# The joints of four interleaved attention layers: loads, row buffers and last rows moved

## The chip, the cores and the metric

The kernel runs on one core of one Trainium2 chip. The core has five engines: TensorE (PE, matrix products into PSUM), VectorE (DVE), ScalarE (ACT), GpSimd (POOL) and SyncE (SP), which here only issues DMAs. The metric is the device time of one execution in microseconds (us); less is better. A profile shows one execution on a time scale that starts with the span.

## The reference

2048 tokens of width 640 pass through four residual layers, A, B, A, B. Each adds the layer's output to its input, after a normalization of rows.

```python
x = x + _A_ref(_layernorm(x), A_wq, A_wk, A_wv, A_wo, A_beta)
x = x + _B_ref(_layernorm(x), B_mem0, B_Wq, B_Wk, B_Wv, B_Wo, B_seg_len)
x = x + _A_ref(_layernorm(x), A_wq, A_wk, A_wv, A_wo, A_beta)
x = x + _B_ref(_layernorm(x), B_mem0, B_Wq, B_Wk, B_Wv, B_Wo, B_seg_len)

# A: 32 heads of 20, four segments of 512 tokens
for s in range(4):
    p = softmax(q @ k.T * scale + mask)                 # causal, within the segment
    a_mem = (phi(q) @ M) / (phi(q) @ z + 1e-06)          # memory of the segments before
    o = sigmoid(beta) * a_mem + (1 - sigmoid(beta)) * (p @ v)
    M, z = M + phi(k).T @ v, z + sum(phi(k))
# then o @ wo

# B: 32 heads of 128, 64 steps of 32 tokens, 8 memory rows
for s in range(64):
    h = concat(mem, x[32 * s:32 * s + 32])               # 40 rows
    p = softmax(mask(q @ k.T * scale))                   # q, k, v from h
    o = (p @ v) @ Wo
    mem, out = o[:8], o[8:]                              # mem goes into the next step
```

## The kernel before

**Layer A** (`layer_A`) takes a segment of 512 tokens and 8 groups of 4 heads, 32 groups in all. Four row tiles of 128 tokens are loaded (`seg_load`, a_xt), normalized (`seg_norm`: bn_stats, a_ln_rstd, a_xn), transposed on PE (`seg_tr`, a_tps to a_xnT) and projected (`proj_q`: a_QP, `proj_kv`: a_KV). `unread` issues PE products a_W that nobody reads; they keep PE at work while it waits. The output of a segment is stored by `out_stage_b`: the product a_YP, the residual row a_xr added on DVE (a_xnew), the sum stored in f32 (xres), cast to bf16 (a_xnb) and stored again (xres_bf). PE's order is that of the program; `KeyOrder` orders DVE, ACT and POOL by due times, `K.base` plus an entry of `A_LAGS`. The padded weights of layer A (a_wq_pad, a_wkv) are made by DVE casts in the first layer, kept in HBM (`keep_padded`) and loaded from there in the second A layer.

**Layer B** (`layer_B`) has the query and key weights resident. The value weights (W.wv) and output weights (b_wo, eight loads of 640 KB) are loaded for each B layer. For the token rows, which don't depend on the memory, queries, keys and values are made ahead in tiles, `tail_unit` (b_tail, evacuated to b_tu, stored through b_QKd) and `vtail_unit` (b_vtail, stored through b_VTd, loaded again as b_Vth). A step s makes Ka, Qa, Kb, Qb for the eight memory rows, transposes them (b_TPak, b_TPaq, b_TPbk, b_TPbq), forms scores (b_SP), softmax on DVE, ACT and POOL, the transposed probabilities (b_PTa, b_PTb), PV (b_OTP, evacuated to b_OTsb), and the output product b_OPS. b_OPS covers the 24 leading tokens of the step and the 8 memory rows; the 8 last tokens of the steps are put aside (b_OTdef) and multiplied for four steps together in `od_chunk` (b_OPSd). `x_out` adds two halves of the product to the residual rows on DVE (b_XO, b_XOd for the put-aside rows, b_XOe for those of the last four steps) and stores. The queries of the memory rows give the next memory; after the last step there is none. All engines but SP follow the program's order here (`_OrdNC`).

**SP** issues nearly all DMAs, in one queue whose order the scheduler decides. A buffer that is reused makes its next writer wait for the last reader. Pools give the addresses: a pool's tile can take over the place of tiles of the layer before, as a_xt takes W.wv's place at the B to A joint.

The lines that the change touches most: the one a_xnb buffer and its two stores,

```python
nc.sync.dma_start(x_dst[r0:r0 + 128, :], xnew[:])
xnb = w1l.tile([128, D], BF16, name="a_xnb")
nc.scalar.copy(xnb[:], xnew[:])                      # last segment; before, on POOL
nc.sync.dma_start(xb_dst[r0:r0 + 128, :], xnb[:])
```

and the end of layer B, after the last step:

```python
for _ in range(4):
    od_chunk()
od_end()
```

## Time and profile before

| | us |
|---|---|
| median of 3 runs | 2575.98 (2574.44 to 2577.28) |
| the profiled execution | 2574.74 |
| its span | 2573.0 |
| PE busy in it | 2486.0 (97%) |
| DVE, ACT, POOL busy | 1675.5, 1519.1, 696.2 |
| first A layer, first b_Ka of the first B layer | 0 to 383.3 |
| first B layer, from there to the last b_Vb's end | to 1276.5 |
| second A layer and its joints, to the second b_Ka | to 1681.7 |
| second B layer | to 2573.0 |

In the rows of the timeline the first two numbers are the start and the duration in us, then come engine (SPq is SP's DMA queue, PEld the weight load of PE), line, operation, output and inputs, the tile's form, how many instructions were taken together, and in brackets the time that the engine stood idle before, with what ended the idle time. A wait row gives the total, the count and the longest one. In the rows of windows stand the bounds, the length, then for PE, PEld, DVE, ACT and POOL the busy time and the instructions, then PE's granted clock (1.00 is full), the share of the DMA engines that were busy, and GB/s. PE's busy time includes the products that nobody reads.

### The profile page before, as it was taken

The numbers are of one execution on the slowest core, as the hardware profiler recorded it, in microseconds if no ns is written. First come the engines' busy times: TensorE is split into PE (matmuls) and PEld (weight loads), VectorE is DVE, ScalarE is ACT, GpSimd is POOL, SyncE is SP. The second block draws the span as 40 slices with busy tenths as digits, with TensorE's granted clock in tenths as the row PEclk, the third lists the DMA queues.
The fourth block names the chain that finished last, engine by engine and source line by source line (L and its number), as shares of the span: only waits on it lengthen the run. The fifth ranks groups of instructions, "written<-read, shape, count | busy, mean of one in ns | idle before, by whom it ended". The sixth has DMA issues, their size and how long they took to land.

```text
span 2573.0 us, 139432 instructions
## 1 busy us (share of the span) xinstructions
PE 2486.0 (97%) x62088; PEld 1639.1 (64%) x62088; DVE 1675.5 (65%) x4597; ACT 1519.1 (59%) x3430; POOL 696.2 (27%) x1471
## 2 busy tenths in 40 slices
PE   7999999999999999999989999999999999999998
PEld 5666576666666666666655665766666666666665
DVE  8999845565556556555579998455655655555555
ACT  6999945555555545444369999445554555555443
POOL 5677621111111111111146776111111111111110
PEclk9999999999999999999999999999999999999999
DMA  4122372222222222121220212721212122111111
GB/s 158 46 85 78 91 239 45 50 48 44 51 45 48 46 50 46 39 39 29 63 84 17 68 53 86 233 47 43 45 41 50 42 45 47 42 42 34 38 26 21
DMA packets 325308, 157.18 MB, mean 61 GB/s; under 512 B 244960, under 2 KB 309600, under 8 KB 322912
## 3 DMA queue, kind: packets, MB, share of 16 engines
q1 hardware_dynamic: 324704, 148.26, 22.1%
q8 instruction: 485, 7.95, 1.3%
q14 instruction: 119, 0.97, 0.1%
HBM read 96.46 MB, written 51.71 MB: 58 GB/s over the span
## 4 chain that ended last, share of the span: by engine, by line
PE 78%; DVE 10%; ACT 8%; issue 2%; DMA 1%; POOL 1%; SPq 0%; ACTq 0%; DVEq 0%; POOLq 0%
PE b_OPS L110 11%; PE b_tail L110 6%; PE b_Ka L110 5%; PE b_Kb L110 5%; PE b_Qa L110 5%; PE b_Qb L110 5%; PE b_Va L110 5%; PE b_Vb L110 4%; DVE a_nm L139 4%; PE b_SP L110 4%; ACT a_PT L139 4%; PE b_vtail L110 3%; PE b_OPSd L110 3%; PE b_OTP L110 3%; PE a_S L110 2%
## 5 line engine op out<-in xcount | busy, mean ns | idle before, releaser
L110 PEld LDWEIGHTS <-b_HX 128*32 128x32 bf16 x15360 | 427.8, 96 | 331.3 <-issue 1.3
L110 POOL TENSOR_TENSOR b_Pn<-b_E,b_rs 128x200 bf16<-128x200 bf16 x128 | 78.0, 609 | 1332.7 <-PE b_Vb L110 1016.9
L139 DVE TENSOR_REDUCE a_nm<-a_S 128x2 f32<-128x512 f32 (+3 forms) x512 | 395.0, 816 | 53.1 <-PE a_S L110 38.1
L139 ACT ACTIVATE a_PT<-a_T 128x1024 bf16<-128x1024 f32 (+1 forms) x384 | 345.8, 904 | 28.3 <-PE a_T L110 21.0
L110 PE MATMUL b_OPS<-b_wo,b_OTsb 128*32 128x320 bf16 x8192 | 303.1, 300 | 1.6 <-issue 0.5
L110 PEld LDWEIGHTS <-b_OTsb 128*32 128x32 bf16 x8192 | 205.7, 96 | 76.3 <-DVE b_OTsb L110 3.3
L139 POOL TENSOR_SCALAR_AFFINE_SELECT a_PT<-a_PT 128x256 bf16<-128x256 bf16 x380 | 188.5, 501 | 154.7 <-ACT a_PT L139 153.4
L110 DVE CAST b_HX<-b_MT 128x8 bf16<-128x8 f32 x372 | 63.6, 172 | 234.0 <-PE b_MT L110 228.3
L110 ACT CAST b_msb<-b_OPS 128x64 bf16<-128x64 f32 x378 | 69.5, 256 | 223.7 <-PE b_OPS L110 223.6
L110 ACT CAST b_kq<-b_Kb 128x512 bf16<-128x512 f32 x128 | 74.9, 585 | 201.4 <-PE b_Kb L110 201.4
L110 DVE COPY b_KT<-b_TPak 128x128 bf16<-128x128 bf16 x128 | 28.7, 224 | 228.2 <-PE b_TPak L110 228.2
L110 DVE TENSOR_SCALAR b_kq<-b_Qa 128x512 bf16<-128x512 f32 x128 | 88.5, 691 | 120.1 <-PE b_Qa L110 116.8
L110 PE MATMUL b_Va<-b_wv,b_HX 128*32 128x512 bf16 x2520 | 161.0, 380 | 0.0
L110 PEld LDWEIGHTS <-b_kq 128*128 128x128 bf16 x2080 | 116.8, 98 | 69.4 <-ACT b_kq L110 56.4
L110 PE MATMUL b_Vb<-b_wv,b_HX 128*32 128x512 bf16 x2520 | 160.7, 379 | 0.0
L110 PE MATMUL b_Ka<-b_wk,b_HX 128*32 128x512 bf16 x2520 | 159.1, 379 | 0.1
L110 PE MATMUL b_Qb<-b_wq,b_HX 128*32 128x512 bf16 x2520 | 158.6, 379 | 0.0
L110 PE MATMUL b_Kb<-b_wk,b_HX 128*32 128x512 bf16 x2520 | 158.6, 379 | 0.0
L110 PE MATMUL b_Qa<-b_wq,b_HX 128*32 128x512 bf16 x2520 | 158.6, 379 | 0.0
L110 DVE CAST b_OTsb<-b_OTP 128x160 bf16<-128x160 f32 (+1 forms) x384 | 130.5, 376 | 38.8 <-PE b_OTP L110 34.6
L110 ACT CAST b_kq<-b_Ka 128x512 bf16<-128x512 f32 x128 | 74.9, 585 | 108.9 <-PE b_Ka L110 108.9
L110 PE MATMUL b_vtail<-b_wv,b_TX 128*32 128x256 bf16 x2880 | 133.9, 271 | 2.4 <-issue 2.3
(206 smaller groups left out, 5432.5 us busy)
## 6 DMA issues: line engine op xcount, KB each, us to landing
b_QKd<-b_tu SPq DMA_DIRECT2D x128, 128.0 KB
b_tl<-b_QKd SPq DMA_DIRECT2D x64, 256.0 KB
b_wv<-in_B_Wv_dram SPq DMA_DIRECT2D x10, 1024.0 KB
b_wo<-in_B_Wo_dram SPq DMA_DIRECT2D x16, 640.0 KB
b_Vth<-b_VTd SPq DMA_DIRECT2D x512, 16.0 KB
b_XO<-xres SPq DMA_DIRECT2D x256, 30.0 KB
b_VTd<-b_vt SPq DMA_DIRECT2D x224, 32.0 KB
b_xt<-xres_bf SPq DMA_DIRECT2D x40, 160.0 KB
```

Source lines behind the costliest of these rows:

```text
L110: r = f(*a, **k)
L139: r = f(*a, **k)
```

## The change

At the start: the load of beta is issued first, its exp and the gate values are computed before the statistics of the first rows, which now wait for the constants' casts; the due times of the first segment's four tiles are spread (1.2 apart instead of 0.1).

At the A to B joints: the last segment's bf16 rows get four buffers in one a_Onat tile instead of one; the third and fourth residual rows are loaded with the first two, into a_no tiles. In the built order the ten YP products of the third and fourth row tile stand earlier on PE, and the b_wo loads earlier on SP, between the stores of b_tu.

At the B to A joint and at the end: the last step makes no Qa and Qb and no transposes of them (their columns are set to zero by POOL). The last step's own 8 trailing tokens are part of its b_OPS instead of the put-aside rows, so those cover three steps; the 80 put-aside products and both their `x_out`s come before OTP and b_OPS. Some stores of the last step are issued by ACT, and so is the load of a_wkv in the second A layer, behind ACT's last instruction of layer B. In the last B layer the put-aside rows of the end have a store buffer of their own.

```diff
@@ -70,7 +70,7 @@
         for i in range(2):
-            nc.vector.tensor_copy(C.negu[:, i, :], neguf[:])
+            C.after_consts = nc.vector.tensor_copy(C.negu[:, i, :], neguf[:])
         nc.vector.memset(C.pad[:], 0.0)
@@ -211,6 +211,7 @@
         nc.sync.dma_start(bb[:], A_beta.partition_broadcast(128))
+    yield
     e = pool.tile([128, 32], F32, name="a_beta_e")
@@ -221,7 +222,7 @@
 
-def load_A_weights(nc, W, A_wq, A_wk, A_wv, A_wo, padded, stage):
+def load_A_weights(nc, tc, C, W, A_wq, A_wk, A_wv, A_wo, padded, stage):
 
@@ -229,7 +230,8 @@
         nc.sync.dma_start(W.wq[:].rearrange("p c h s -> p (c h s)"), padded["wq"])
-        nc.sync.dma_start(W.wkv[:].rearrange("p c g n -> p (c g n)"), padded["wkv"])
+        f = nc.scalar.dma_start(W.wkv[:].rearrange("p c g n -> p (c g n)"), padded["wkv"])
+        tc.add_manual_dep(f.ins, C.act_last.name, mybir.DependencyInfo(mybir.DependencyClass.NoSync, mybir.DependencyReason.SCHED_ONLY), reason="order")
     nc.sync.dma_start(W.wo[:], A_wo.rearrange("(c p) n -> p c n", p=128))
@@ -330,7 +332,9 @@
             for i in range(2):
-                K("st").vector.bn_stats(out=stats[:, i, :], in_=xt[:, 320 * i:320 * i + 320])
+                f = K("st").vector.bn_stats(out=stats[:, i, :], in_=xt[:, 320 * i:320 * i + 320])
+                if src_is_bf16 and n_ + tt + i == 0:
+                    tc.add_manual_dep(f.ins, C.after_consts.ins.name, K.info, reason="order")
             mv = sml.tile([128, nc.vector.BN_AGGR_DIM], F32, name="a_ln_mv", tag="ln_mv")
@@ -366,9 +370,6 @@
             r0 = n_ * 512 + tt * 128
-            if xr is None:
-                xr = wkl.tile([128, D], BF16 if src_is_bf16 else F32, name="a_xr")
-                nc.sync.dma_start(xr[:], x_src[r0:r0 + 128, :])
             if n_ == nseg - 1 and (tt or not src_is_bf16):
@@ -383,12 +384,17 @@
             nc.sync.dma_start(x_dst[r0:r0 + 128, :], xnew[:])
-            xnb = w1l.tile([128, D], BF16, name="a_xnb")
             if n_ == nseg - 1:
-                nc.scalar.copy(xnb[:], xnew[:])
+                if tt == 0:
+                    d["xnb"] = pon.tile([128, 4, D], BF16, name="a_Onat", tag="Onat")
+                xnb = d["xnb"][:, tt, :]
             else:
-                K("xnb").gpsimd.tensor_copy(xnb[:], xnew[:])
-            nc.sync.dma_start(xb_dst[r0:r0 + 128, :], xnb[:])
+                xnb = w1l.tile([128, D], BF16, name="a_xnb")[:]
+            if n_ == nseg - 1:
+                nc.scalar.copy(xnb, xnew[:])
+            else:
+                K("xnb").gpsimd.tensor_copy(xnb, xnew[:])
+            nc.sync.dma_start(xb_dst[r0:r0 + 128, :], xnb)
 
@@ -449,7 +455,7 @@
             if step not in NOs:
-                NOs[step] = wk.tile([128, 2, 4, 4, 21], F32, name="a_no")
+                NOs[step] = wk.tile([128, 2, 4, 4, 21], F32, name="a_no", tag="a_no")
             return NOs[step]
@@ -608,13 +614,15 @@
 
+        gates = build_gates(nc, st, W, side_loads[1]) if side_loads is not None else iter(())
+        next(gates, None)
         for tt in range(4):
...
         for tt in range(4):
-            K.base = 0.1 * tt - 100.0
+            K.base = 1.2 * tt - 100.0
             seg_norm(0, tt)
@@ -632,6 +640,7 @@
         K.base = None
+        next(gates, None)
         unread(4)
@@ -689,9 +698,9 @@
                         d["tps"] = d.get("tps", []) + [psx.tile([128, 2, 2 * 512], BF16, name="a_otps", tag="x")]
-                    xr = wkl.tile([128, D], BF16 if src_is_bf16 else F32, name="a_xr") if tt < 2 else None
-                    if tt < 2:
-                        nc.sync.dma_start(xr[:], x_src[512 * nseg - 512 + 128 * tt:512 * nseg - 384 + 128 * tt, :])
+                    dt_ = BF16 if src_is_bf16 else F32
+                    xr = wkl.tile([128, D], dt_, name="a_xr") if tt < 2 else wk.tile([128, D], dt_, name="a_xr2", tag="a_no")
+                    nc.sync.dma_start(xr[:, 0:D], x_src[512 * nseg - 512 + 128 * tt:512 * nseg - 384 + 128 * tt, :])
                     d["xr"][tt] = xr
@@ -737,8 +746,6 @@
                     if side_loads is not None and g < NGR:
-                        if g + half + ph == 0:
-                            build_gates(nc, st, W, side_loads[1])
                         side_loads[0](4 * g + 2 * half + ph, GS[g]["kT"])
@@ -1050,7 +1057,7 @@
             if out_bf16:
-                xo = wk.tile([64, 320], BF16, name=f"b_xnb{nm}", tag=f"xnb{nm}")
+                xo = (bx if nm == "e" else wk).tile([64, 320], BF16, name=f"b_xnb{nm}", tag="tl" if nm == "e" else f"xnb{nm}")
             else:
@@ -1059,16 +1066,19 @@
                 for jj2 in range(2):
-                    nc.sync.dma_start(d_half(x_dst[32 * s:32 * s + 24, :], jj2), xo[32 * jj2:32 * jj2 + 24, :].rearrange("t (c x) -> t c x", x=64))
+                    for r0, t0, t1 in (((0, 0, 24),) if s < nsteps - 1 else ((8, 0, 24), (0, 24, 32))):
+                        r_ = 32 * jj2 + r0
+                        (nc.scalar if jj2 and s == nsteps - 1 else nc.sync).dma_start(d_half(x_dst[32 * s + t0:32 * s + t1, :], jj2), xo[r_:r_ + t1 - t0, :].rearrange("t (c x) -> t c x", x=64))
             return f
...
             x_ = x_dst if store else x_src
+            n_ = min(4, nsteps - 1 - s0) if store else 4
             for jj2 in range(2):
-                sb = xo[32 * jj2:32 * jj2 + 32, :].rearrange("t (c x) -> t c x", x=64)
-                dr = x_[32 * s0:32 * s0 + 128, :].rearrange("(i t) (c j x) -> i t j c x", t=32, j=2, x=64)[:, 24:32, jj2]
+                sb = xo[32 * jj2:32 * jj2 + 8 * n_, :].rearrange("t (c x) -> t c x", x=64)
+                dr = x_[32 * s0:32 * s0 + 32 * n_, :].rearrange("(i t) (c j x) -> i t j c x", t=32, j=2, x=64)[:, 24:32, jj2]
                 if store:
-                    nc.sync.dma_start(dr, sb)
+                    (nc.scalar if n_ < 4 else nc.sync).dma_start(dr, sb)
                 else:
@@ -1085,8 +1095,8 @@
 
-        def od_end():
-            x_out(od["ps"], od["xo"], lambda xo: tail_dma(od["s0"], True, xo), "d")
+        def od_end(od=od, nm="d"):
+            x_out(od["ps"], od["xo"], lambda xo: tail_dma(od["s0"], True, xo), nm)
             od.clear()
@@ -1109,7 +1119,9 @@
             for jj2 in range(2):
-                nc.sync.dma_start(XO[32 * jj2:32 * jj2 + 24, :].rearrange("t (c x) -> t c x", x=64), d_half(x_src[32 * s:32 * s + 24, :], jj2))
+                for r0, t0, t1 in (((0, 0, 24),) if not last else ((0, 24, 32), (8, 0, 24))):
+                    r_ = 32 * jj2 + r0
+                    nc.sync.dma_start(XO[r_:r_ + t1 - t0, :].rearrange("t (c x) -> t c x", x=64), d_half(x_src[32 * s + t0:32 * s + t1, :], jj2))
 
@@ -1173,26 +1185,32 @@
             ka = kq(Ka, "act")
-            Qa = thin_mm(cols, W.wq, 0, "b_Qa")
-            qa = kq(Qa, "dve", SCB)
+            if last:
+                nc.gpsimd.memset(QT[s][:, :, 24:32], 0.0)
+            else:
+                Qa = thin_mm(cols, W.wq, 0, "b_Qa")
+                qa = kq(Qa, "dve", SCB)
             Kb = thin_mm(cols, W.wk, 1, "b_Kb")
             kb = kq(Kb, "act")
-            Qb = thin_mm(cols, W.wq, 1, "b_Qb")
-            qb = kq(Qb, "act", SCB)
+            if not last:
+                Qb = thin_mm(cols, W.wq, 1, "b_Qb")
+                qb = kq(Qb, "act", SCB)
 
...
             x_scatter(TPak, 0, KT)
-            TPaq = transp4(qa, "b_TPaq")
-            scatter("dve", TPaq, 0, QT[s], 0, 8, 24)
-            x_scatter(TPaq, 0, QT)
+            if not last:
+                TPaq = transp4(qa, "b_TPaq")
+                scatter("dve", TPaq, 0, QT[s], 0, 8, 24)
+                x_scatter(TPaq, 0, QT)
             TPbk = transp4(kb, "b_TPbk")
...
             SPa = mask_mm(0)
-            TPbq = transp4(qb, "b_TPbq", po.tile([128, 4, 128], BF16, name="b_TPbq", tag="tail"))
-            scatter("dve", TPbq, 1, QT[s], 0, 8, 24)
-            x_scatter(TPbq, 1, QT)
+            if not last:
+                TPbq = transp4(qb, "b_TPbq", po.tile([128, 4, 128], BF16, name="b_TPbq", tag="tail"))
+                scatter("dve", TPbq, 1, QT[s], 0, 8, 24)
+                x_scatter(TPbq, 1, QT)
             SPb = mask_mm(1)
@@ -1221,6 +1239,12 @@
                 tail_evac(unit[0], unit[1], "act")
+            if last:
+                od_chunk()
+                oda = dict(od)
+                od_begin(s - 3, XOe, "tail")
+                for _ in range(4):
+                    od_chunk()
             otf = [ps_tile([128, 2, 4, 40] if j else [128, 4, 40], F32, "b_OTP") for j in range(4)]
@@ -1237,11 +1261,14 @@
                 vtails_in(s + 1)
+            if last:
+                od_end(oda)
+                od_end(nm="e")
             od_chunk(0)
...
             for n_, (j, a) in enumerate(order):
-                o_mm(ops, lambda h: OTsb[:, 40 * h + 8:40 * h + 40], [16 * a + 4 * j + 2 * ip for ip in range(2)], n_ == 0, n_ == 7)
+                o_mm(ops, lambda h: OTsb[:, 40 * h + 8 - 8 * last:40 * h + 40 - 8 * last], [16 * a + 4 * j + 2 * ip for ip in range(2)], n_ == 0, n_ == 7)
             od_chunk(1)
@@ -1275,11 +1302,8 @@
                 od_end()
-                if last:
-                    od_begin(s - 3, XOe, "tail")
-                else:
-                    tail_dma(s - 3, False, XOd)
-                    od_begin(s - 3, XOd)
+                tail_dma(s - 3, False, XOd)
+                od_begin(s - 3, XOd)
             elif s == 3:
@@ -1287,13 +1311,12 @@
             x_out(ops, XO, store_head(s), "")
-            nc.gpsimd.tensor_copy(OTdef[(s // 4) % 2][:, :, 8 * (s % 4):8 * (s % 4) + 8], OTsb[:].rearrange("p (h c) -> p h c", c=40)[:, :, 0:8])
+            if not last:
+                nc.gpsimd.tensor_copy(OTdef[(s // 4) % 2][:, :, 8 * (s % 4):8 * (s % 4) + 8], OTsb[:].rearrange("p (h c) -> p h c", c=40)[:, :, 0:8])
             if ln_due(s + 1):
...
             QT.pop(s, None); KT.pop(s, None); VH.pop(s - 1, None)
-        for _ in range(4):
-            od_chunk()
-        od_end()
+        C.act_last = nc._prox["scalar"]._last
 
@@ -1324,7 +1347,7 @@
                 layer_A(nc, tc, C, WA, xin if first else X, X, first, xb_dst=Xb,
-                        load_w=lambda: load_A_weights(nc, WA, A_wq, A_wk, A_wv, A_wo, padded, stage),
+                        load_w=lambda: load_A_weights(nc, tc, C, WA, A_wq, A_wk, A_wv, A_wo, padded, stage),
                         side_loads=(side, A_beta) if first else None)
```

## The prediction

> **What bounds the kernel now.** The page comes first. TensorE (PE) is busy for 97% of the span, so in the long middle of each layer nothing but less PE work, or PE work better fed, shortens the run.
>
> ```profile
> span 2573.0 us, 139432 instructions
> PE 2486.0 (97%) x62088; PEld 1639.1 (64%) x62088; DVE 1675.5 (65%) x4597; ACT 1519.1 (59%) x3430; POOL 696.2 (27%) x1471
> ```
>
> The missing 87 us are thin waits inside layer A and a few long ones where one layer hands over to the next. The change touches only the start, the three joints and the end, so I read the waits of PE in a window around each, and the timeline of PE, DVE (VectorE), ACT (ScalarE) and SP's queue there. The middle of a B layer is the yardstick: the step that starts with this Ka and the last one, 62 steps later (row in the part on the end, 2551.01), are (2551.01 - 1681.65) / 62 = 14.02 us apart.
>
> ```profile
> 1681.65 1.25 PE L110 MATMUL b_Ka<-b_wk,b_HX 128*32 128x512 bf16 x20
> ```
>
> The instruction order built from the changed kernel is the same as before on every engine inside the A segments and the B steps; it differs at the five places below. I cost them one by one, against the profiled execution: span 2573.0, its own time 2574.74. The median of the runs, 2575.98, lies 1.24 above that, and I add the same 1.24 at the end. No change can be told from one of under 0.2%, 5.2 us.
>
> **Start.** Columns: start, duration, engine, operation, and in brackets the idle time before with its releaser.
>
> ```profile
> 0.81 1.81 SPq L324 DMA_DIRECT2D a_xt<-in_A_x_dram  x4
> 9.45 0.73 SPq L213 DMA_DIRECT2D a_beta_bf<-in_A_beta_dram  x1
> 3.19 0.89 DVE L139 BATCH_NORM_STATS2 a_ln_st<-a_xt 128x6 f32<-128x320 bf16 x2
> 8.23 0.36 DVE L73 CAST c_negu<-c_neguf 128x128 bf16<-128x128 f32 x2
> 14.28 0.99 DVE L139 COPY a_wkv<-b_wq 128x3200 bf16<-128x3200 bf16 x1 [0.32 <-DMA b_wq<-in_A_wv_dram]
> 17.01 0.23 ACT L215 ACTIVATE a_beta_e<-a_beta_bf 128x32 f32<-128x32 bf16 x1 [0.74 <-DMA a_beta_bf<-in_A_beta_dram]
> 17.27 0.18 DVE L216 TENSOR_SCALAR a_beta_e<-a_beta_e 128x32 f32<-128x32 f32 x1 [1.99 <-ACT a_beta_e L215]
> 17.39 1.21 PE L110 MATMUL a_KV<-a_wkv,a_xnT 128*128 128x160 bf16 x13
> ```
>
> DVE is one unbroken string from 3.19 to 15.27, and KV, the first real work that needs the value weights, starts at 17.39. Now beta's load is issued ahead of x: x lands 0.73 later, 3.9. Beta took 7.6 us behind the weights; alone in front, I give it x's 2.4 us (0.81 to 3.19): there at 3.2, exp 0.23, six gate operations of some 0.18 to 0.35 (1.1 in all), then the identity and negu casts (0.5, moved forward, not added) which now stand ahead of the statistics: statistics start near 5.5. The rest of the string is 12.08 less 0.5 for the moved casts and 0.32 for the wait that the later position covers: 11.3, so the last cast ends near 16.7. KV follows it at once instead of 2.1 us after, because the rows' normalizations are now interleaved with the statistics, so that the transposes ahead of KV are done sooner. 16.8 against 17.39: gain 0.6 (bounds: -1 if beta is 1.6 later, +2 if KV is freed as early as the cast was, 15.3).
>
> **First A to B joint.**
>
> ```profile
> 349.14 0.72 ACT L388 CAST a_xnb<-a_xnew 128x640 bf16<-128x640 f32 x1 [2.15 <-DMA xres_bf<-a_xnb]
> 353.34 0.72 ACT L388 CAST a_xnb<-a_xnew 128x640 bf16<-128x640 f32 x1 [3.47 <-DMA xres_bf<-a_xnb]
> 354.61 0.38 PE L110 MATMUL b_tail<-b_TX,b_wq 128*128 128x128 bf16 x4 [1.90 <-ACT b_tu L110]
> 378.95 0.50 PE L110 MATMUL b_vtail<-b_wv,b_TX 128*32 128x256 bf16 x9 [1.45 <-issue]
> ```
>
> There is one bf16 row buffer (a_xnb), so ACT stands twice until its store has landed, and the evacuations (b_tu) behind it on ACT hold PE for 1.90. With four slots the casts wait for nothing. What takes the wait's place: the slots lie in the memory of a_Onat, which b_tu of later tiles and POOL's memset of QZ reuse; they now wait for the four stores. The third cast could start with the second at 349, as nothing but the adds delays it, so I put the last landing near 350 to 351, ahead of 353.34, where ACT stood until now. I choose to leave 0.2 of the 1.90 for that. Loads of the residual rows now stand on SP ahead of layer B's first x loads and wait for a buffer of POOL's; layer A's last units cover it, and if they did not, it is in the lower bound. The 1.45 of "issue" I leave as it is. Gain 1.7 (bounds 0.8, half the stall left, and 1.9 + 1.45 = 3.4).
>
> **B to A joint.**
>
> ```profile
> 1269.07 1.25 PE L110 MATMUL b_Qa<-b_wq,b_HXz 128*32 128x512 bf16 x20
> 1270.15 1.25 PE L110 MATMUL b_Kb<-b_wk,b_HXz 128*32 128x512 bf16 x20
> 1276.56 1.77 SPq L324 DMA_DIRECT2D a_xt<-xres  x4
> 1277.61 0.38 PE L110 MATMUL b_OTP<-b_PTa,b_Vth 32*128 32x40 bf16 x32 [1.08 <-DVE b_PTa L110]
> 1280.73 2.62 PE L110 MATMUL b_OPSd<-b_wo,b_OTdef 128*32 128x320 bf16 x72
> 1279.52 0.89 DVE L139 BATCH_NORM_STATS2 a_ln_st<-a_xt 128x6 f32<-128x320 f32 x2 [0.36 <-DMA a_xt<-xres]
> 1286.52 0.49 DVE L110 TENSOR_TENSOR b_XO<-b_OPS,b_XO 64x320 f32<-64x320 f32 x1
> 1287.07 1.03 PE L110 MATMUL a_W<-c_negu,c_identb 128*128 128x256 bf16 x6 [3.72 <-DVE a_ln_rstd L139]
> 1291.05 0.50 SPq L232 DMA_DIRECT2D a_wkv<-a_wkv_home  x1
> 1298.31 2.85 PE L110 MATMUL a_KV<-a_wkv,a_xnT 128*128 128x160 bf16 x20 [4.31 <-DMA a_wkv<-a_wkv_home]
> ```
>
> The last step loses Qa and Qb (1270.15 - 1269.07 = 1.08 each) and two sets of four transposes. I take 2.05 for the score path, a little less than the 2 x 1.08, since Kb's evacuation on ACT then is what comes last. 80 deferred products (2.62 x 80/72, some 2.8) go in front of OTP, so OTP starts near 1277.1, half a us earlier. That is not what sets the joint: PE then waits 3.72 for the last output add, which frees its accumulator. On DVE the statistics of the next layer's first two tiles now stand ahead of the evacuations of OTP. Their loads go out when the value weights are done, 2.05 earlier, so x lands near 1277.45 and those statistics end at 1277.45 + 2 x 1.23 (0.89 and two small operations) = 1279.9; then come three evacuations, one normalization, six adds of about 0.48 and the other statistics, and the last XO add ends near 1287.0, as now (1286.52 + 0.49). So a_W and QP stay where they are. What moves is a_wkv: it was issued behind three pairs of stores on SP and took 7.2 us; on ACT's queue it stands behind ACT's stores, of which the last wait for that XO add: two issues of some 0.7 after 1287.0 (the stores at the end, quoted below, take 1.37 for two), and a little for the adds' own order: 1288.7. It lands, at 7.2, at 1295.9: KV 2.4 earlier, all of it in the 4.31 that PE stands. Bounds: 0 (wo, which SP now issues beside it, takes half of the engines' time), and 4.3 (it never is last).
>
> ```profile
> 1288.00:1292.00 4.00, 4.00 (x35) 3.45 (x34) 3.39 (x7) 2.08 (x3) 3.02 (x6) 0.63 0.22 46
> 1296.00:1300.00 4.00, 1.69 (x13) 1.70 (x14) 0.00 (x0) 0.14 (x1) 0.00 (x0) 0.73 1.00 383
> 1304.73 0.86 PE L110 MATMUL a_KV<-a_wkv,a_xnT 128*128 128x160 bf16 x10
> ```
>
> In these windows the last three numbers are granted clock, DMA share and GB/s. The DMA engines stand at 0.22 before the load and at 1.00 during it, so an earlier issue uses free time. The clock fell to 0.63 after the first stall and to 0.73 in the second; 20 KV matmuls took 2.85 where twice the later row makes 1.7. The Trainium skill ("TensorE: Matmul & The Clock Gate", Part 1) says that the clock halves only after an idle window of about 3.4 us; a gap cut to 1.9 would then also save the slow KV, an estimate of 1.1 more, 2561.7 at the end instead of 2562.8. The trace agrees that the clock falls after gaps of 3.72 and 4.31; I keep the smaller gain.
>
> **Second A to B joint.**
>
> ```profile
> 1632.03 1.52 PE L110 MATMUL a_YP<-a_wo,a_oT 128*128 128x320 bf16 x10 [1.27 <-DVE a_xnew L139]
> 1631.48 0.89 DVE L139 TENSOR_TENSOR a_xnew<-a_YP,a_xr 128x320 f32<-128x320 f32 x2 [3.97 <-DMA a_xr<-xres]
> 1636.59 0.38 SPq L779 DMA_DIRECT2D b_wo<-in_B_Wo_dram  x1
> 1658.98 4.46 SPq L1112 DMA_DIRECT2D b_XO<-xres  x1
> 1675.94 0.55 PE L110 MATMUL b_OTP<-b_PTa,b_Vth 32*128 32x40 bf16 x30 [1.19 <-DMA b_Vth<-b_VTd]
> 1676.93 3.89 PE L110 MATMUL b_OPS<-b_wo,b_OTsb 128*32 128x320 bf16 x64
> 1278.56 2.35 PE L110 MATMUL b_OPS<-b_wo,b_OTsb 128*32 128x320 bf16 x64
> 1630.00:1642.00 12.00, 10.30 (x165) 9.55 (x163) 8.20 (x18) 3.52 (x6) 2.74 (x5) 1.00 0.62 200
> 1642.00:1660.00 18.00, 17.97 (x404) 15.20 (x404) 7.27 (x14) 6.74 (x13) 0.00 (x0) 1.00 0.97 319
> ```
>
> The third and fourth residual rows get a buffer late, so DVE waits 3.97 and PE 1.27; they are now loaded with the others: 1.27 gone. The output weights (b_wo) go out behind the last row stores at 1636.59; with four row buffers and the adds done, near 1631.6, 5 us earlier, into a window with 0.38 x 12 = 4.6 us of free transfer time. They saturate the engines until 1660, hold SP for 4.46 at b_XO, and so bring Vth late: a PE wait of 1.19, just after one of 0.30, and 64 OPS matmuls at a lower clock, 3.89 against 2.35. PE itself comes 1.7 earlier, so 5 - 1.7 = 3.3 against a lateness of 1.5 (the sum of the waits): hidden, with 1.8 to spare. Gain 1.27 + 1.49 + 1.54 = 4.3 (bounds: 1.3, when only the first goes, and 4.7: PE stood 1.70 in the first of the two windows, 0.43 more than the 1.27).
>
> **End.**
>
> ```profile
> 2551.01 0.82 PE L110 MATMUL b_Ka<-b_wk,b_HXz 128*32 128x512 bf16 x12
> 2568.67 0.49 DVE L110 TENSOR_TENSOR b_xnbd<-b_OPSd,b_XOe 64x320 bf16<-64x320 f32 x1 [1.39 <-DMA out_dram<-b_xnbd]
> 2569.19 1.37 SPq L1071 DMA_DIRECT2D out_dram<-b_xnbd  x2
> ```
>
> Here no next layer competes for DVE. At the other last step OTP started 8.54 after Qa, so here near 2551.01 + 1.08 + 8.54 = 2560.6; with half a us gained, 2560.1. Evacuation 0.9, OPS 2.35: 2563.4; two adds of 0.49: 2564.4; stores on SP and ACT side by side, two issues each of 0.7: near 2566.0 to 2566.4. The deferred products and their adds lie ahead of that, in the gap before OTP. The span ended 2573.0 - 2570.56 = 2.4 after the last issue: 2568.8. Gain 4.2 (bounds 3 and 5: one issue more or less, and the wait of 1.39 for the buffer, which is gone, back as a wait of ACT).
>
> **Sum.** 0.6 + 1.7 + 2.4 + 4.3 + 4.2 = 13.2: 2574.74 - 13.2 = 2561.5 for a profiled execution, 2562.8 for the median.
>
> **The rivals.** *DVE holds the B to A joint* (0.13). Statistics that wait for x stand ahead of OTsb. If x lands not 2.96 after its issue but some 5 (four tiles and wq are in flight at once), OTsb and the last add, and with it a_wkv's issue, come 2 to 4 us later: the joint gives 0 to -2, time 2565.2 to 2567.2. Against it: the first tile did take 2.96 with the same loads behind it.
>
> *Earlier weights collide at the A to B joints* (0.14). The same bytes at share 0.97 must still pass; if the eight wo loads now delay the row stores and QKd, the evacuations stall as before, and Vth stays late: 0.8 and 2.0 are left of 1.7 and 4.3, time 2566.0. The 1.45 of "issue" in b_vtail fell in such a saturated stretch, and can grow. The Trainium skill ("Runtime: NRT & Kernel Launch", Instruction fetch mechanics) has instruction blocks fetched by DMA, the cost mostly hidden; that row, with no other releaser, does not look hidden.
>
> *Beta is slow even in front* (0.05): after 7.6 us, as now, DVE's string would start at 9.9: the start loses 3.8 instead of gaining 0.6, time 2567.2.
>
> *Slower: the B steps lengthen* (0.06). The row buffers, the tails' buffers and a_Onat's memory change place. If in the steps one store or tail load then lands after its reader asks, each step gains one wait. 124 steps (twice 62) times 0.11 us eats the 13.2; over 0.15 the kernel is measurably slower. At 0.2, somewhat above that point, it is 24.8: 2587.6. Against it: the order and the waits within steps are those of before.
>
> **How the numbers follow.** The sum as forecast has 0.62; its own bounds give about 2557 to 2567. The three mild rivals end at 2565.2 to 2567.2, and two at once near 2571: so the range is 2556 to 2570. Faster by over 0.2% is below 2570.8: the forecast and nearly all of the mild rivals, 0.88; 0.06 within 0.2%, where mild rivals add up; 0.06 slower.
>
> **What would show it.** Right: b_tail's wait on b_tu under 0.5; no wait of OTP on Vth after the second A segment, and OPS there near 2.4; KV's wait for a_wkv near 2; the last store issue ending before 2567 on the old scale. Wrong: a step longer than 14.1 us, PE waiting for OTsb over 2 us at the B to A joint, or KV later than 10 us after a_W's start at 1287.

## The result and the profile after

The changed kernel takes 2561.37 us, median of 4 runs (2558.34 to 2564.21), against 2575.93 (2574.44 to 2577.28) for the kernel before: ratio 0.9943, 95% interval 0.9926 to 0.9961. The forecast was 2562.8, faster. On another chip, where everything ran longer, it was 2566.53 against 2584.57 (0.9933, 0.9919 to 0.9947). The profiled execution is the fastest of the four, 2558.34, so its span is shorter by 16.4 us where the medians differ by 14.6.

The page of the changed kernel; PE is as busy as before, and a second DMA queue (q10, ACT's) carries 1.79 MB:

```profile
span 2556.6 us, 139246 instructions
PE 2477.6 (97%) x61992; PEld 1631.8 (64%) x61992; DVE 1672.4 (65%) x4591; ACT 1518.7 (59%) x3428; POOL 695.5 (27%) x1471
...
q10 hardware_dynamic: 996, 1.79, 0.2%
```

Where the 16.4 us came from is read by matching one instruction at each boundary in both timelines. The last a_otps, the a transpose ahead of the last output products, marks the end of a layer A; step 1's Ka and the last Ka mark the steps of a layer B.

| stretch | before | after | gain | forecast |
|---|---|---|---|---|
| start, to the first layer's last a_otps | 339.57 | 337.87 | 1.70 | 0.6 |
| first A to B joint, to Ka of step 1 | 57.79 | 54.84 | 2.95 | 1.7 |
| steps of the first B layer, to its last Ka | 870.63 | 870.10 | 0.53 | 0 |
| B to A joint and second A layer, to its last a_otps | 353.83 | 352.88 | 0.95 | 2.4 |
| second A to B joint, to Ka of step 1 | 59.83 | 54.11 | 5.72 | 4.3 |
| steps of the second B layer, to its last Ka | 869.36 | 868.73 | 0.63 | 0 |
| last step, to the end of the span | 21.99 | 18.07 | 3.92 | 4.2 |
| sum | 2573.00 | 2556.60 | 16.40 | 13.2 |

The timeline of the changed kernel at the start (start, duration, engine, operation, idle time before and its releaser):

```profile
3.78 0.23 ACT L216 ACTIVATE a_beta_e<-a_beta_bf 128x32 f32<-128x32 bf16 x1 [1.07 <-DMA a_beta_bf<-in_A_beta_dram]
5.52 0.88 DVE L139 BATCH_NORM_STATS2 a_ln_st<-a_xt 128x6 f32<-128x320 bf16 x2
9.55 0.44 DVE L139 TENSOR_SCALAR a_xn<-a_xt,a_ln_mv,a_ln_rstd 128x640 bf16<-128x640 bf16 x1
15.81 1.56 PE L110 MATMUL a_KV<-a_wkv,a_xnT 128*128 128x160 bf16 x20 [0.66 <-DVE a_wkv L139]
```

Statistics start at 5.52, as forecast (5.5). KV comes at 15.81, not 16.8.

The B to A joint of the changed kernel, DVE, PE and ACT's DMA queue:

```profile
1272.79 0.89 DVE L139 BATCH_NORM_STATS2 a_ln_st<-a_xt 128x6 f32<-128x320 f32 x2 [2.20 <-DMA a_xt<-xres]
1271.85 0.38 PE L110 MATMUL b_OTP<-b_PTa,b_Vth 32*128 32x40 bf16 x32
1275.62 0.72 PE L110 MATMUL b_OPS<-b_wo,b_OTsb 128*32 128x320 bf16 x8 [3.08 <-DVE b_OTsb L110]
1277.23 3.93 PE L110 MATMUL b_OPS<-b_wo,b_OTsb 128*32 128x320 bf16 x56 [0.88 <-DVE b_OTsb L110]
1282.67 0.83 PE L110 MATMUL a_W<-c_negu,c_identb 128*128 128x256 bf16 x6 [1.51 <-DVE b_XO L110]
1284.30 0.74 ACTq L233 DMA_DIRECT2D a_wkv<-a_wkv_home  x1
1292.44 2.85 PE L110 MATMUL a_KV<-a_wkv,a_xnT 128*128 128x160 bf16 x20 [3.10 <-DMA a_wkv<-a_wkv_home]
```

DVE waits for x, then does the statistics of two tiles, and only then evacuates OTP, which has been ready since 1272.5. PE waits 3.08 and 0.88 for these evacuations and then runs OPS at a low clock (3.93 for 56 products, where 64 took 2.35 before). KV still waits for its weights, 3.10 instead of 4.31.

The second A to B joint:

```profile
1620.51 1.52 PE L110 MATMUL a_YP<-a_wo,a_oT 128*128 128x320 bf16 x10
1628.37 0.38 SPq L786 DMA_DIRECT2D b_wo<-in_B_Wo_dram  x1
1659.38 2.90 SPq L934 DMA_DIRECT2D b_Vth<-b_VTd  x4
1665.71 0.37 PE L110 MATMUL b_OTP<-b_PTa,b_Vth 32*128 32x40 bf16 x32
1666.55 2.43 PE L110 MATMUL b_OPS<-b_wo,b_OTsb 128*32 128x320 bf16 x64
```

The ten YP products have no wait, OTP none for Vth, and OPS takes 2.43 instead of 3.89. Vth is issued 6.3 us ahead of its reader, where its last wait before was 1.19.

The end:

```profile
2551.70 0.49 DVE L110 TENSOR_TENSOR b_xnb<-b_OPS,b_XO 64x320 bf16<-64x320 f32 x1
2552.87 1.60 ACTq L110 DMA_DIRECT2D out_dram<-b_xnb  x2
```

The last issue ends at 2554.47; the span ends 2.1 after it (2.4 before).

### The profile page after: what moved, and what is told of

The parts are those of the page before. It is cut to its first block, busy times and chain, and to the rows that moved or that the text cites. A ratio compares the mean times of both kernels' runs of the same rounds, so it can differ in the third digit from the quotient of the medians.

```text
span 2556.6 us, 139246 instructions
## 1 busy us (share of the span) xinstructions
PE 2477.6 (97%) x61992; PEld 1631.8 (64%) x61992; DVE 1672.4 (65%) x4591; ACT 1518.7 (59%) x3428; POOL 695.5 (27%) x1471
## 3 DMA queue, kind: packets, MB, share of 16 engines
q10 hardware_dynamic: 996, 1.79, 0.2%
## 4 chain that ended last, share of the span: by engine, by line
PE 79%; DVE 10%; ACT 7%; issue 1%; DMA 1%; POOL 1%; SPq 0%; ACTq 0%; DVEq 0%; POOLq 0%
PE b_OPS L110 11%; PE b_tail L110 7%; PE b_Ka L110 5%; PE b_Kb L110 5%; PE b_Qb L110 5%; PE b_Qa L110 5%; PE b_Va L110 5%; PE b_Vb L110 5%; DVE a_nm L139 4%; PE b_SP L110 4%; ACT a_PT L139 4%; PE b_vtail L110 3%; PE b_OPSd L110 3%; PE b_OTP L110 3%; PE a_S L110 2%; PE b_TPak L110 2%
```

## The experiments

The first theory behind the joint that gave least: DVE's order there, not the loads, took the gain, and a_wkv on ACT's queue is late because it stands behind ACT's last stores. The rival: the loads bind, and the queue helped. All kernels below are the changed kernel with the edit shown.

The kernels of the evacuations, of a_wkv on SP, of the memset and of the kept queries ran once each, on a chip where the kernel before took 2581.14 in its one run: 2553.41, 2558.12, 2562.08 and 2560.85. The others ran on a chip where it took 2584.57: one row buffer 2571.68 and the late residual rows 2577.91, once each, and both repairs and the changed kernel five times each (below). Times of different chips are not compared; the readings go by stretches within a trace, from an instruction that all traces have. "The changed kernel" without more is the trace above.

**Evacuations first.**

```diff
+                C.after_evac = nc._prox["vector"]._last        # last step, after the evacuations of OTP
...
-                if src_is_bf16 and n_ + tt + i == 0:
-                    tc.add_manual_dep(f.ins, C.after_consts.ins.name, K.info, reason="order")
+                if n_ + tt + i == 0:
+                    tc.add_manual_dep(f.ins, C.after_consts.ins.name if src_is_bf16 else C.after_evac.name, K.info, reason="order")
```

> The changed kernel with one order added: at the B to A joint the statistics of the second A layer's first rows wait on DVE until the last step's evacuations of OTP are done. Theory (DVE's order took the joint's gain): in the changed kernel DVE stood 2.20 us for x while OTP was ready, PE then stood 3.08 and 0.88 us before OPS, and the last output add and with it the issue of a_wkv came late. With the evacuations first, PE's waits for b_OTsb fall under 0.5 us together, a_W's first start moves from 1282.7 to about 1277, QP from 1288.1 to about 1284.6, KV from 1292.4 to 1286 to 1288; gain 3.5 to 6 us. Rival (the joint is bound by its loads): x, the query weights and a_wkv pass the DMA engines at their limit, so KV moves by less than 1 us.

```profile
1271.99 2.38 PE L110 MATMUL b_OPS<-b_wo,b_OTsb 128*32 128x320 bf16 x64 [0.15 <-DVE b_OTsb L110]
1276.59 0.83 PE L110 MATMUL a_W<-c_negu,c_identb 128*128 128x256 bf16 x6 [2.23 <-DVE a_ln_rstd L139]
1284.80 1.60 PE L110 MATMUL a_QP<-a_xnT,a_wq_pad 128*128 128x512 bf16 x5
1287.70 0.87 PE L110 MATMUL a_KV<-a_wkv,a_xnT 128*128 128x160 bf16 x10 [1.30 <-DMA a_wkv<-a_wkv_home]
```

The waits for b_OTsb went from 3.96 to 0.15, a_W came at 1276.6 (forecast 1277), QP at 1284.8 (1284.6), KV at 1287.7. From the last Ka to KV it took 25.59 us instead of 29.63, and to the end of the stretch in the table 348.04 instead of 352.88. The output adds came ahead of most statistics too: from the last Ka to a_W it took 14.48, and 14.48 again in the kernel with both repairs below, where five traces with the order of the changed kernel have 18.58 to 19.86. DVE's order is shown to hold the joint; the loads hold a rest of 1.30.

**a_wkv on SP's queue.**

```diff
-        f = nc.scalar.dma_start(W.wkv[:].rearrange("p c g n -> p (c g n)"), padded["wkv"])
-        tc.add_manual_dep(f.ins, C.act_last.name, ...)
+        nc.sync.dma_start(W.wkv[:].rearrange("p c g n -> p (c g n)"), padded["wkv"])
```

> The changed kernel with the load of a_wkv back on SP's queue, where the scheduler puts it right behind the query weights and ahead of the stores. Theory (ACT's queue, behind ACT's last stores, is the late place): the load is issued near 1272.5 instead of 1284.3 and lands before QP ends, so PE's wait of 3.1 us for it goes; QP stays near 1288.1, KV starts near 1289.2 and its 20 products take less than the 2.85 us; gain 3 to 4.5 us. Rival (the move to ACT's queue is what helped): on SP the load lands later than 1292.4, or takes bandwidth from x and the query weights so that QP comes over 1 us later; no gain or a loss.

```profile
1275.05 0.44 SPq L233 DMA_DIRECT2D a_wkv<-a_wkv_home  x1
...
1290.76 1.24 PE L110 MATMUL a_QP<-a_xnT,a_wq_pad 128*128 128x512 bf16 x5 [0.34 <-ACT a_xnT L139]
1291.84 0.85 PE L110 MATMUL a_KV<-a_wkv,a_xnT 128*128 128x160 bf16 x10
```

In this run the last Ka was at 1265.34, 2.53 later than in the changed kernel, so the time as a whole shows no gain: 2.03 went in the first layer, where the granted clock stood at 0.50 from 36 to 39 us, and 1.51 at the first joint (a stall that the part on one row buffer comes back to). The load is issued 9.7 us after the last Ka (21.5 in the changed kernel), PE does not wait for it, and KV starts 26.50 after the last Ka instead of 29.63 (27.32 in the changed kernel's repeat below), 1.08 after QP instead of 4.34. To the last a_otps the gain is 2.35 of the 3.1; 3 to 4.5 were forecast. So ACT's queue, with its order behind the stores, was the late place for this load: in the same program SP has a place 12 us earlier.

**Both repairs, and beside them the changed kernel again.**

> The changed kernel with both repairs of the B to A joint: the evacuations of OTP ahead of the next layer's statistics on DVE, and a_wkv on SP's queue behind the query weights. Theory (two separate lateness, of DVE's string and of the load): from the last Ka to KV 29.63 us in the changed kernel, 25.59 with the first repair, 26.50 with the second; with both PE never waits for a_wkv, KV starts about 24 after the last Ka, and the run is 5 to 7 us shorter than the changed kernel's. Rival (both repairs remove the same time): about 4 us, no more than the first alone.

> The changed kernel once more, beside the repaired one. Both theories: 2558 to 2564 us, with the scatter coming from where TensorE's clock is granted in full after the stalls of the second A layer's start; the rival of a fixed time would have the runs within 1.5 us of each other.

```profile
1286.86 1.24 PE L110 MATMUL a_QP<-a_xnT,a_wq_pad 128*128 128x512 bf16 x4 [0.19 <-DMA xres<-b_XO]
1287.94 1.69 PE L110 MATMUL a_KV<-a_wkv,a_xnT 128*128 128x160 bf16 x20
```

With both, KV starts 23.76 after the last Ka (at 1264.18), and the stretch to the last a_otps is 347.31. Runs: 2557.42 (2556.31 to 2561.21) against 2566.53 (2564.52 to 2568.14) for the changed kernel and 2584.57 for the kernel before; ratio to the latter 0.9903 (0.9886 to 0.9919). The two ranges do not meet. The repaired kernel is faster than both; between the medians lie 9.1 us, where 5 to 7 were forecast. The changed kernel itself was forecast at 2558 to 2564 and lay above that, on a chip where the kernel before was slower too. The two latenesses are separate, as the theory had it, though they do not add in full: 352.88 less 4.84 and 2.35 would be 345.7. Of the difference of 10.2 us between these two profiled spans, 6.2 lie in this stretch; 3.9 lie in B steps, whose order and waits the repairs do not touch, so some of the 9.1 us may be scatter.

The repeat's stretches, in the order of the table, are 337.86, 55.43, 872.83, 353.47, 54.30, 872.76 and 18.05. The changed kernel's five runs spread over 3.6 us, and its stretch from the last Ka to the last a_otps took 353.47 here, 352.88 before, and 353.59, 353.83 and 354.29 in three experiments that leave that place's order alone or nearly so; in a fourth 356.50. The 0.95 gained there lies within this scatter. One source of it, in two windows of the granted clock (the last three numbers are clock, DMA share, GB/s), the changed kernel first:

```profile
1292.00:1296.00 4.00, 3.39 (x28) 3.13 (x28) 0.00 (x0) 1.16 (x5) 0.00 (x0) 0.57 0.22 85
1296.00:1300.00 4.00, 3.48 (x35) 1.95 (x34) 2.85 (x4) 1.42 (x4) 0.45 (x1) 1.00 0.00 0
```

and the kernel with the memset moved (below), which at this joint is the changed kernel:

```profile
1292.00:1296.00 4.00, 3.58 (x29) 3.15 (x28) 0.00 (x0) 1.85 (x6) 0.46 (x1) 0.50 0.04 12
1296.00:1300.00 4.00, 4.00 (x16) 1.18 (x16) 1.82 (x2) 0.59 (x1) 0.00 (x0) 0.50 0.00 0
```

After the same wait for a_wkv (3.10 and 3.15) the clock came back at about 1295 in one run and 1300 in the other, and from KV's start to the last a_otps the second took 325.32 instead of 323.24, 2.1 us more. The repeat of the changed kernel shows the same loss behind a shorter wait:

```profile
1293.44 0.87 PE L110 MATMUL a_KV<-a_wkv,a_xnT 128*128 128x160 bf16 x10 [2.12 <-DMA a_wkv<-a_wkv_home]
1298.18 2.31 PE L110 MATMUL a_QP<-a_xnT,a_wq_pad 128*128 128x512 bf16 x5
1294.00:1301.00 7.00, 6.40 (x36) 3.40 (x35) 1.82 (x2) 2.66 (x8) 0.45 (x1) 0.52 0.14 55
1458.00:1462.00 4.00, 3.78 (x24) 1.67 (x28) 3.61 (x6) 2.28 (x4) 3.50 (x8) 0.57 0.00 0
```

KV starts 27.32 after the last Ka there, 2.3 earlier than in the first trace, but the clock is low behind it and once more in mid-layer, and the way to the last a_otps takes 326.15. With evacuations first, where the clock is 1.00 from KV on (1288 to 1340), it takes 322.44. So what the joint gains at KV can be lost again to the clock behind it.

**POOL's memset beside the normalizations.** Why did the start give 1.70 and not 0.6?

```diff
             f = K("pow").gpsimd.tensor_tensor(...)
+            if n_ == 0 and src_is_bf16 and tt == 1:
+                C.first_pow = f
...
-        nc.gpsimd.memset(W.wq[:, :, :, 20:32], 0.0)
+        f = nc.gpsimd.memset(W.wq[:, :, :, 20:32], 0.0)
+        tc.add_manual_dep(f.ins, C.first_pow.ins.name, K.info, reason="order")
```

> The changed kernel with POOL's memset of a_wq_pad put behind the second of the first four powers at the start, where DVE normalizes rows beside it. Theory (the start gained 1.7 instead of 0.6 us because POOL's long memset no longer runs beside DVE's normalizations, which took 0.82 us each beside it and 0.44 without): the second or third a_xn takes over 0.8 us instead of 0.44, and KV starts 0.4 to 1.5 us later than 15.8. Rival (the gain is from the spread order of statistics and normalizations alone): every a_xn stays within 0.1 us of its time and KV within 0.3 us.

The kernel before, and then this one:

```profile
9.82 1.87 POOL L236 MEMSET a_wq_pad<- 128x1920 bf16 x1
9.98 1.89 DVE L139 TENSOR_SCALAR a_xn<-a_xt,a_ln_mv,a_ln_rstd 128x640 bf16<-128x640 bf16 x1
...
8.75 1.69 POOL L238 MEMSET a_wq_pad<- 128x1920 bf16 x1
...
9.53 1.09 DVE L139 TENSOR_SCALAR a_xn<-a_xt,a_ln_mv,a_ln_rstd 128x640 bf16<-128x640 bf16 x1
11.76 0.44 DVE L139 TENSOR_SCALAR a_xn<-a_xt,a_ln_mv,a_ln_rstd 128x640 bf16<-128x640 bf16 x1
```

The a_xn under the memset took 1.09, the next one 0.44, and KV came at 16.91 instead of 15.81; the first layer's last a_otps is 1.17 later. The a_xn ended 0.18 after the memset, as the fourth a_xn of the kernel before did (11.87 against 11.69; the 0.82 each of the expectation is the mean of 0.44, 0.73, 0.45 and 1.89). The first cast behind the normalizations started 0.83 later (13.37 against 12.54); the other 0.27 of KV's 1.10 are a longer last cast (1.39 against 1.13), which the run with a_wkv on SP has too, without the memset. So most of the extra gain of the start is the memset, which now runs while DVE does the statistics.

**Queries of the last step kept.** Edit: the four branches on `last` around Qa, Qb and their transposes always taken.

> The changed kernel with the last step's queries of the memory rows made again (Qa, Qb, their evacuations and transposes). Theory (at the B to A joint DVE binds, at the end PE's string does): at the joint a_W and KV move by less than 0.6 us against the last Ka, since x and the evacuations behind it set OPS; at the end the span grows by about 2.6 us (two times 1.08 and eight transposes). Rival: the dropped products are worth the same 2.6 us in both places.

From the last Ka, OTP starts 2.21 later (11.25 instead of 9.04) at the B to A joint, but KV 0.46 earlier (29.17 instead of 29.63), inside the 27.32 to 29.73 of the traces with that joint's order unchanged: no worth of the dropped products can be seen there. From the last Ka to the end of the span it took 20.06 instead of 18.07: they are worth 2.0 at the end. The theory was right on the places; the 2.6 was too high by 0.6.

**One row buffer; late residual rows.** What carries the A to B joints?

```diff
-                if tt == 0:
-                    d["xnb"] = pon.tile([128, 4, D], BF16, name="a_Onat", tag="Onat")
-                xnb = d["xnb"][:, tt, :]
+                xnb = w1l.tile([128, D], BF16, name="a_xnb")[:]
```

> The changed kernel with one bf16 row buffer for the last segment again (the residual rows still loaded early). From the last transposes of layer A to step 1's Ka the changed kernel took 54.84 us at the first A to B joint and 54.11 at the second; the kernel before 57.79 and 59.83. Theory (the row buffers carry the first joint, and at the second the start of the output weights, and so Vth's lateness, hangs on them): b_tail waits 1.5 to 2 us for b_tu again at the first joint, the stretch is longer by 1.7 to 2.8 us there; at the second the first b_wo is issued 2 to 5 us later and the stretch is longer by 2 to 4.5 us. Rival (the early residual rows carry the second joint): the first joint as above, the second longer by under 1 us.

First joint 57.88 instead of 54.84 (+3.04; forecast 1.7 to 2.8), second 56.31 instead of 54.11 (+2.20; 2 to 4.5). Neither difference is all the edit's. The rows of the first joint, and below them the same stall in the changed kernel, in its repeat and with a_wkv on SP:

```profile
353.05 3.51 PE L110 MATMUL b_tail<-b_TX,b_wq 128*128 128x128 bf16 x60 [1.68 <-ACT b_tu L110]
353.08 0.38 SPq L784 DMA_DIRECT2D b_wo<-in_B_Wo_dram  x1
378.10 0.51 PE L110 MATMUL b_vtail<-b_wv,b_TX 128*32 128x256 bf16 x10 [2.17 <-issue]
...
374.61 0.51 PE L110 MATMUL b_vtail<-b_wv,b_TX 128*32 128x256 bf16 x10 [0.95 <-issue]
375.18 0.50 PE L110 MATMUL b_vtail<-b_wv,b_TX 128*32 128x256 bf16 x10 [1.54 <-issue]
378.14 0.51 PE L110 MATMUL b_vtail<-b_wv,b_TX 128*32 128x256 bf16 x10 [2.44 <-issue]
```

The b_tail wait is back, 1.68. The stall that the trace puts down to "issue" varies by itself: 0.62 to 2.44 in the seven traces that leave this joint's order alone, 1.45 before. Less that stall, the first joint takes 53.9 to 54.0 in all seven, 55.7 here and 56.3 before: one row buffer costs 1.8, as forecast.

At the second joint OTP does not wait for Vth, so the theory's path is not seen. YP waits 1.39 for DVE and b_tail 0.65 for b_tu, but the wait of YP also comes without the edit; here in this run, and with the memset moved:

```profile
1625.64 0.84 PE L110 MATMUL a_YP<-a_wo,a_oT 128*128 128x320 bf16 x5 [1.39 <-DVE a_xr L139]
1620.36 0.84 PE L110 MATMUL a_YP<-a_wo,a_oT 128*128 128x320 bf16 x5 [1.60 <-DVE a_xr L139]
```

In the seven traces it is between nothing and 1.60, and the stretch 53.81 to 55.59; less this wait the stretch is 53.7 to 54.2 in them and 54.9 here. That is 0.7 to 1.2 for the row buffer, nearer to the rival (under 1) than to the theory.

The residual rows, with the four buffers kept:

```diff
+            if xr is None:
+                xr = wkl.tile([128, D], BF16 if src_is_bf16 else F32, name="a_xr")
+                nc.sync.dma_start(xr[:], x_src[r0:r0 + 128, :])
...
-                    xr = wkl.tile(...) if tt < 2 else wk.tile([128, D], dt_, name="a_xr2", tag="a_no")
+                    xr = wkl.tile(...) if tt < 2 else None
```

> The changed kernel with the third and fourth residual rows of the last segment loaded late again (four row buffers kept). Theory: at the second joint YP waits about 1.3 us for the adds again and the last row store, and with it the first b_wo, comes 2 to 5 us later, so the stretch from the last transposes to step 1's Ka is longer by 1.3 to 3 us than the 54.11 of the changed kernel; at the first joint, where the residual rows come from the input and the wait of 1.43 was not on PE's path, by under 0.6. Rival (b_wo's start hangs on the row buffers alone): the second joint longer by 1.3 at most, with Vth not waited for.

The second joint took 57.68 (+3.57, or +3.38 on the repeat's 54.30; forecast 1.3 to 3), with a wait of 0.58 for Vth and the lowered clock in OPS again; b_tail waits 0.80 for b_tu. The 1.3 on YP that I expected did not come back, and b_wo's first load came 13.64 after the last a_otps, where the changed kernel has 12.69 and I had 2 to 5 later.

```profile
1677.29 0.36 PE L110 MATMUL b_OTP<-b_PTa,b_Vth 32*128 32x40 bf16 x29 [0.58 <-DMA b_Vth<-b_VTd]
1679.28 3.28 PE L110 MATMUL b_OPS<-b_wo,b_OTsb 128*32 128x320 bf16 x48 [0.33 <-ACT b_OTsb L110]
```

The first took 58.84 (+4.00), where under 0.6 was forecast:

```profile
353.34 0.38 SPq L790 DMA_DIRECT2D b_wo<-in_B_Wo_dram  x1
371.21 0.40 PE L110 MATMUL b_TP<-c_identb,b_kq 128*128 128x128 bf16 x4 [0.74 <-DVE b_kq L110]
378.33 0.51 PE L110 MATMUL b_vtail<-b_wv,b_TX 128*32 128x256 bf16 x10 [2.47 <-issue]
378.57 4.12 PE L110 MATMUL b_V<-b_wv,b_HX 128*32 128x512 bf16 x40
```

No wait on PE goes back to the late rows themselves. But the last two YPs and their stores come later, and b_wo's first load with them: 14.06 us after the last a_otps, where the changed kernel has 10.94 (348.81). The stall on "issue" is 2.47, at the top of its range, and the products after it (4.12 where 2.43 is usual) lose clock, as they did not after the 2.44 shown above. Less the stall the joint takes 56.4, 2.5 more than the seven traces: 1.69 of it is the clock, 0.74 the wait of b_TP. The place of the output weights' loads does not explain the stall: with b_wo's first load 10.5 to 11.1 after the last a_otps it was 0.62 to 2.44, and in the kernel before, with that load at 15.03, it was 1.45. Its cause stays open.

## Why the prediction held, and where its steps were off

**Start: direction right, size too small.** Beta landed in time, statistics at 5.52 against 5.5. The step that failed is the length of DVE's string behind it: 11.3 us forecast, taken over from the rows of before; it was 10.24 (5.52 to 15.76). The last normalization in those rows had run beside POOL's memset, 1.89 instead of 0.44. The order in which POOL stood was in reach; I moved the instructions and left their durations.

**First A to B joint: right, too small.** The 1.90 went entirely (I had left 0.2). The 1.45 of "issue", costed at nothing, fell to 0.95, which was luck: in other traces of the same order that stall is 0.62 to 2.44. Without it the joint gained 2.45 (56.34 to 53.89); the rest beyond the 1.90 is mostly small PE waits (0.29 on b_lntps, 0.15 on b_OTsb). The bound of 3.4 held.

**B to A joint: the step that failed.** I put the statistics ahead of the evacuations correctly, took from it that a_W and QP stay, and gave a_wkv's earlier issue all of the gain. From the last Ka, a_W came 0.78 later than before (19.86 against 19.08), QP 0.52 later; a_wkv was issued 1.57 earlier, not 2.35, and took 8.1 us, not the 7.2 of its row. KV came 0.69 earlier where I had 2.4, and 0.95 is left in the table. One trace is not enough for these sizes. In the five with this joint's order (the two of the changed kernel, and those with the memset moved, one row buffer and late residual rows) a_W comes at 18.6 to 19.9, a_wkv takes 6.9 to 8.5, and KV is 0.6 to 3.0 earlier than before; the stretch in the table still takes 352.9 to 356.5, against 353.8. So a_W's place was right (19.1 forecast), and KV's term had the right sign and, over the five, some 1.5 of its 2.4: a_wkv mostly took longer than its one row. What failed altogether is the step from KV to the end of the stretch: I let KV's gain pass whole. That part took 323.5 before and 323.2 to 326.8 in the five, where 322.4 is possible; the clock, which I had left as it was, is low there for longer in most of them. And PE waits 3.5 to 4.1 for b_OTsb in all five, over the 2 that I had named as a sign of being wrong: the place of a_W that I took as given was DVE's order.

The rival that DVE holds the joint, which had 0.13, came nearer in its time (0 to -2) and was right on the engine, not on the way: x did not take 5 us but 2.9 to 3.8, and a_wkv's issue was 0.3 earlier to 0.8 later than I had it, not 2 to 4 later. The order alone holds it, as the first experiment shows.

The extra step with the clock did not come either: the Trainium skill ("TensorE: Matmul & The Clock Gate", Part 1) would have the KV products at full speed after a gap under about 3.4 us, and after 3.10 they took 2.85, as slow as after 4.31. Two traces have a gap near the 1.9 that I meant, 2.12 in the repeat and 2.00 with the queries kept:

```profile
1291.97 1.71 PE L110 MATMUL a_KV<-a_wkv,a_xnT 128*128 128x160 bf16 x20 [2.00 <-DMA a_wkv<-a_wkv_home]
1294.00:1300.00 6.00, 5.69 (x28) 2.71 (x29) 2.62 (x3) 1.67 (x5) 0.45 (x1) 0.50 0.00 0
```

The first KV products are fast there, and then the granted clock falls to 0.50 all the same. The measurement decides: a gap of 2 us did not keep the clock at this place.

**Second A to B joint: right, too small.** 5.72 against 4.3, above my upper bound of 4.7. YP's 1.27, Vth's 1.49 and 1.46 of OPS are all gone. Of the two parts of the change, the early residual rows carry more of this joint: without them it is 3.4 to 3.6 longer, with one row buffer some 1. What I left out were the small PE waits around them: 0.23 and 0.20 on b_tu, 0.30 on "issue", 0.29 on b_lntps. I bounded the sum from one window, and they lay in several. One wait of YP on a_xr, not there before and 0.39 here, moves between nothing and 1.60 from trace to trace, so the size is not sharper than that.

**End: right.** 3.92 against 4.2; half of it (2.0) is the dropped products, by experiment.

**The sum** was right partly because errors of both signs met: 1.1, 1.3 and 1.4 too little, 1.5 and 0.3 too much, and 1.2 of B steps that no step forecast and that are of the size of scatter: four traces of one chip, whose edits leave these steps alone, have 868.8 to 870.2 and 868.2 to 869.7 there, the repeat on the other chip 872.8 in both. The slower rival did not come: B steps are 13.98 apart in the middle, 13.99 before.

## What to carry to other kernels

When a step is shortened at a hand-over between layers, look first at which engine's queue holds the next layer's work ahead of the last layer's: here statistics that waited for a load stood ahead of evacuations that were ready, and one order brought the next layer's first products forward by 4 to 5 us. A load moved to another engine's queue inherits that queue's waits; ask where it would stand in the queue that it left once the rest of the change is made. Durations taken from a trace hold for the neighbours that they had there.

## What was not expected of the hardware

DVE's normalization of 128x640 in bf16 took 0.44 us alone and 1.09 when POOL's memset of 1.69 was under way, and ended 0.18 after it: it was held, not slowed. At the first A to B joint of the kernel before the same form took 1.78 beside three memsets in a row (354.03 to 355.72), and again ended 0.18 after the last. The Trainium skill ("SBUF — State Buffer", Who interferes with whom) states that such DVE operations can need a pair of ports that DVE shares with POOL, and that whoever is first holds it for the whole instruction; these numbers agree.

After the same stall of PE, of 3.10 and 3.15 us, the full clock came back some 5 us apart in two runs of the same instructions, worth 2.1 us. A gain at such a place has to be larger than that, or be taken from several runs.
